# Reordering the tasks, the first transfers and the weight loads of an attention kernel with a woven MLP

## The chip, the cores and the metric

One core of a Trainium2 chip runs the whole program. The metric is the device time of one execution in microseconds (us). The kernel before took 422.31 us, the median of three runs (421.84 to 426.07); the run that was profiled took 421.53.

The engines: TensorE (PE in the profile; PEld is its weight load), VectorE (DVE), ScalarE (ACT), GpSimd (POOL) and SyncE (SP), which here only issues transfers. A suffix q (ACTq, SPq, POOLq) means that engine's sequencer.

## The reference

```python
def _attn_ref(q, k, v, s):            # 8 batches x 8 heads, sequence 576, head size 64
    scores = scale * q @ k^T
    cum = cumsum(max(s, 0))
    scores += minimum(-(cum_i - cum_j), 0), causal
    attn = softmax(scores)
    return attn @ v
def _moe_ref(x, w_in, w_out):         # 4608 tokens, 512 -> 2048 -> 512
    h = x @ w_in
    return (h * clip(h + 3, 0, 6) / 6) @ w_out
```

The output of the attention, all heads of a token side by side, is the input x of the MLP.

## The kernel before

Two heads of one batch form a pair; there are 32. For each pair q and k are loaded in f32, cast to f16 on GpSimd (`cast_qk`), transposed in two groups on TensorE, and copied out of PSUM by VectorE. The scores of a head come in four PSUM banks. ScalarE takes the exponential of each and GpSimd zeroes the upper triangle (`mask`). `attend` multiplies by v, and `x_transpose` writes the normalised result into the MLP's input.

```python
S = psum.tile([128, 512], F32, tag="S", bufs=3)   # score banks, transposes and x transposes share it

def att_tasks(p):
    tasks = []
    def pre():
        if p + 2 < NP: load_aug(p + 2)            # decay rows, read back from DRAM
        if p + 3 < NP: load_pair(p + 3)           # q, k, v
        if p + 1 < NP:
            cast_qk(p + 1)
            cast_v(p + 1)
        for load, c in weights[2 * p:2 * p + 2]:  # eight chunks, pairs 0 to 3, issued by GpSimd
            load(c)
    tasks.append((pre, 0))
    if p + 1 < NP: tasks.append((lambda: transpose_group(p + 1, 0), 640))
    # ... four scores_bank of head 2p, attend(2p - 1)
    # ... transpose_group(p + 1, 1), four scores_bank of head 2p + 1
    # ... x_transpose(p - 1), attend(2p)
```

In the traces here each engine's instructions come in the order in which the program writes them. The attention of pairs 0 to 4 runs alone at the head. Then a weaver mixes attention tasks with MLP tasks by the costs given with the tasks: `m1` is four matmuls into ph, a ReLU on ScalarE (trl) and a product on VectorE; `m2` is four matmuls into po. When attention ends, the MLP runs alone.

The softmax here doesn't subtract the row's maximum and nothing guards it: scores larger than these inputs give would overflow.

## Time and profile before

| Stage | From | To | What runs |
|---|---|---|---|
| head | 0 | 58.0 | loads, attention of pairs 0 to 4; first exponential at 19.8 |
| first weave | 58.0 | 95.0 | pairs 5 to 8 with the first block of m1 |
| rest | 95.0 | 419.6 | attention woven with m1 and m2, then the MLP alone |

The times are where the first ph and the first po start in TensorE's timeline. TensorE is busy for 366.7 of 419.6 us. Nearly all its room is in the first two stages; the lines are in the prediction.

### The profile page before, as it was taken

To read this page: it belongs to the slowest core of one execution; us is meant where nothing else is said; L and a number is where in the kernel's file an instruction comes from. 1 tells how busy PE (TensorE), PEld (TensorE's weight loads), DVE (VectorE), ACT (ScalarE), POOL (GpSimd) and SP (SyncE) were. 2 spreads that over 40 slices of the span, in tenths; PEclk is the share of its full clock that TensorE was granted. 3 is DMA by queue.
4 is the path that set the end of the run, shared out by engine and by line. 5 is a ranking of instruction groups with operands and counts; after the bars stand their busy time and mean duration, and the time that the engine had idled before them with its cause. 6 is when DMAs were issued, how large, how long until landed. Compare 5 with 4: busy or idle time off the path is not lost.

```text
span 419.6 us, 8151 instructions
## 1 busy us (share of the span) xinstructions
PE 366.7 (87%) x3008; PEld 210.0 (50%) x3008; DVE 226.1 (54%) x412; ACT 213.2 (51%) x407; POOL 142.7 (34%) x336
## 2 busy tenths in 40 slices
PE   1274677879999999999999999999999999999985
PEld 0153445545555555555555555555555554444432
DVE  4233346666666666666666666666656644454521
ACT  6153347675555555555555555555555644444400
POOL 3284644444343444444444444444434210000000
PEclk9988589999999999999999999999999999999999
DMA  6999999645554554555555455455501000101011
GB/s 131 166 207 199 200 192 187 124 85 108 111 110 110 111 109 111 111 111 108 111 111 109 111 111 109 112 114 112 110 27 51 26 27 25 52 25 51 25 75 51
DMA packets 123511, 43.38 MB, mean 103 GB/s; under 512 B 114192, under 2 KB 118672, under 8 KB 123472
## 3 DMA queue, kind: packets, MB, share of 16 engines
q1 hardware_dynamic: 119248, 38.68, 42.1%
q0 software_dynamic: 4224, 4.19, 6.3%
q8 instruction: 23, 0.38, 0.4%
q14 instruction: 16, 0.13, 0.1%
HBM read 37.32 MB, written 9.73 MB: 112 GB/s over the span
## 4 chain that ended last, share of the span: by engine, by line
PE 68%; DVE 10%; DMA 6%; ACT 5%; issue 4%; POOL 3%; SPq 3%; POOLq 0%; ACTq 0%
PE po L327 26%; PE ph L309 25%; PE S L203 8%; PE O L252 6%; DVE osb L336 4%; ACT trl L317 3%; DMA t<-in_k_dram 3%; PE pT L163 3%; DVE kT L174 2%; ACT Pm L211 2%; PE pX L277 2%; POOL t L150 2%; DVE qT L173 2%; DMA v_f<-in_v_dram 1%; SPq L132 1%
## 5 line engine op out<-in xcount | busy, mean ns | idle before, releaser
L317 ACT ACTIVATE trl<-ph,bias 128x512 f32<-128x512 f32 x144 | 99.1, 688 | 139.0 <-PE ph L309 138.4
L318 DVE SCALAR_TENSOR_TENSOR gT<-trl,ph 128x512 f16<-128x512 f32 x144 | 99.1, 688 | 99.8 <-ACT trl L317 98.3
L327 PE MATMUL po<-w_out_sb,gT 128*128 128x512 f16 x576 | 144.5, 379 | 2.3 <-DVE osb L336 2.3
L309 PE MATMUL ph<-xT,w_in_sb 128*128 128x512 f16 x576 | 146.3, 379 | 0.0
L216 POOL TENSOR_SCALAR_AFFINE_SELECT Pm<-Pm 128x128 f16<-128x128 f16 (+2 forms) x256 | 78.1, 310 | 168.0 <-ACT Pm L211 156.5
L211 ACT ACTIVATE Pm<-S 128x384 f16<-128x384 f32 (+2 forms) x256 | 112.6, 507 | 44.0 <-PE S L203 43.7
L203 PE MATMUL S<-qT,kT 128*128 128x320 f16 (+4 forms) x448 | 74.2, 273 | 15.6 <-DVE kT L174 9.8
L327 PEld LDWEIGHTS <-gT 128*128 128x128 f16 x576 | 52.2, 98 | 54.7 <-issue 3.2
L309 PEld LDWEIGHTS <-w_in_sb 128*128 128x128 f16 x576 | 51.6, 97 | 52.5 <-issue 9.2
L203 PEld LDWEIGHTS <-kT 128*128 128x128 f16 x448 | 40.4, 102 | 28.7 <-issue 5.5
L173 DVE COPY qT<-pT 64x640 f16<-64x640 f16 x64 | 28.5, 445 | 47.5 <-PE pT L163 47.5
L163 PE MATMUL pT<-ident,t 128*128 128x128 f16 x288 | 28.8, 233 | 26.6 <-POOL t L150 26.6
L252 PEld LDWEIGHTS <-Pm 128*128 128x128 f16 x960 | 40.4, 100 | 17.8 <-POOL Pm L216 4.1
L252 PE MATMUL O<-v_h,Pm 128*128 128x65 f16 x960 | 42.7, 197 | 3.5 <-POOL Pm L216 3.4
L150 POOL CAST t<-t 128x1152 f16<-128x1152 f32 x32 | 37.0, 1158 | 14.9 <-DMA t<-in_k_dram 14.7
L163 PEld LDWEIGHTS <-t 128*128 128x128 f16 x288 | 21.9, 104 | 39.3 <-POOL t L150 27.9
L336 DVE TENSOR_SCALAR osb<-po 128x512 f32<-128x512 f32 x36 | 24.7, 685 | 13.2 <-PE po L327 13.2
L174 DVE COPY kT<-pT 64x640 f16<-64x640 f16 x64 | 29.4, 459 | 0.9
L155 POOL CAST v_h<-v_f 128x640 f16<-128x640 f32 x32 | 23.1, 722 | 12.4 <-DMA v_f<-in_v_dram 11.2
L264 DVE TENSOR_TENSOR xs<-O,r 128x640 f16<-128x640 f32 x32 | 26.4, 824 | 1.1
L262 DVE RECIPROCAL r<-O 128x10 f32<-128x10 f32 x32 | 7.1, 220 | 19.8 <-PE O L252 19.8
L277 PEld LDWEIGHTS <-xs 128*128 128x128 f16 x160 | 11.7, 98 | 11.8 <-issue 5.7
(23 smaller groups left out, 49.1 us busy)
## 6 DMA issues: line engine op xcount, KB each, us to landing
t<-in_q_dram SPq DMA_DIRECT2D x32, 288.0 KB
t<-in_k_dram SPq DMA_DIRECT2D x32, 288.0 KB
out_dram<-osb SPq DMA_DIRECT2D x36, 256.0 KB
v_f<-in_v_dram SPq DMA_DIRECT2D x64, 128.0 KB
w_in_sb<-in_moe_w_in_dram POOLq DMA_DIRECT2D x4, 512.0 KB, 8.7
w_out_sb<-in_moe_w_out_dram POOLq DMA_DIRECT2D x4, 512.0 KB, 8.7
v_f<-in_v_dram SPq DMA_DIRECT2D x32, 32.0 KB
kT<-kaug_scratch SPq DMA_DIRECT2D x32, 6.8 KB
```

The costliest lines, as they stand in the source:

```text
L150: nc.gpsimd.tensor_copy(out=t, in_=qk_f.pop(p))
L163: nc.tensor.matmul(out=pT[:, (t - t0) * 128:(t - t0 + 1) * 128], lhsT=src[:, t, :, :], rhs=ident, is_transpose=True, start=(t == t0), stop ...
L174: nc.vector.tensor_copy(out=kT[0:64, sl, c0:c0 + n], in_=pT[64:128, 0:n])
L203: nc.tensor.matmul(out=S[:, c:c + hi - lo], lhsT=kT[:, sl, off + 128 * kt:off + 128 * (kt + 1)], rhs=qT[:, sl, off + lo:off + hi], start=( ...
L211: nc.scalar.activation(out=P[:, p0:p0 + n], in_=S[:, 0:n], func=AF.Exp, scale=0.125, bias=0.0)
L216: nc.gpsimd.affine_select(out=view, in_=view, pattern=pattern, compare_op=ALU.is_ge, fill=0.0, base=0, channel_multiplier=-1,)
L252: nc.tensor.matmul(out=O[:, hh, qt * VW:qt * VW + D + 1], lhsT=P[:, c:c + 128], rhs=v_h[:, sl, hh, kt, 0:D + 1], start=(qt == 0), stop=(qt ...
L309: nc.tensor.matmul(out=ph, lhsT=w_in_sb[:, kc, f * 128:(f + 1) * 128], rhs=xT[:, kc, n * 512:(n + 1) * 512], start=(kc == 0), stop=(kc == ...
L317: nc.scalar.activation(out=trl, in_=ph, func=AF.Relu, bias=bias3[:, 0:1], scale=1.0)
L318: nc.vector.scalar_tensor_tensor(out=gT[n][:, f, :], in0=trl, scalar=6.0, in1=ph, op0=ALU.min, op1=ALU.mult)
L327: nc.tensor.matmul(out=po, lhsT=gT[n][:, f, t4 * 128:(t4 + 1) * 128], rhs=w_out_sb[:, f, :], start=(f == 0), stop=(f == NF - 1),)
L336: nc.vector.tensor_scalar_mul(out=osb, in0=po, scalar1=1.0 / 6.0)
```

## The change

The diff below is shortened: lines in brackets and `...` stand for what is left out. Its intent is a shorter head and fewer stalls of TensorE before transposes: pair p's scores go ahead of pair p+1's transposes, the cast of q and k goes between the masks, the loads of pairs 1 and 2 are issued before the round trip of the decay rows, part of the first transfers goes to ScalarE's queue, weights load later, and ten zero matmuls are to keep TensorE's clock up. The last line moves the point where the weave begins, so that it still follows `x_transpose`.

```diff
-    nc.sync.dma_start(out=amask[64:128], ...)
-    nc.sync.dma_start(out=ident, in_=ident_dram.ap())
+    nc.scalar.dma_start(out=amask[64:128], ...)
+    nc.scalar.dma_start(out=ident, in_=ident_dram.ap())
 ...
-    load_pair(0)
-    (kaug, qaug written to DRAM by nc.sync)
-    load_aug(0); load_aug(1)
-    load_pair(1); load_pair(2)
+    load_qk(0, nc.sync)
+    load_v(0, nc.scalar)
+    load_qk(1, nc.sync); load_v(1, nc.sync)
+    load_qk(2, nc.sync); load_v(2, nc.sync)
+    mask_rows(0)
+    (kaug, qaug written to DRAM by nc.scalar)
+    mask_rows(1)
+    load_aug(0, nc.scalar); load_aug(1, nc.scalar)
+    mask_rows(2)
 ...
+    for i in range(10):
+        nc.tensor.matmul(out=pw, lhsT=warm[:, 0:128], rhs=warm, ...)
-    weights = [w_in 0..3, w_out 0..3]            # two a pair from pair 0
+    weights = {1: [w_in 0], 2: [w_in 1, w_in 2], 3: [w_in 3],
+               4: [w_out 0, w_out 1], 5: [w_out 2, w_out 3]}
 ...                                              # tasks of pair p, in their new order
+        tasks = [(loads, 0)]
+        for bi in range(4):
+            tasks.append((lambda bi=bi: scores_bank(2 * p, bi), 400))
+            if bi == 1 and more:
+                tasks.append((lambda: cast_qk(p + 1), 0))
+        # attend(2p - 1) at 1200 in place of 1600, then transpose_group(p + 1, 0),
+        # four scores_bank(2p + 1), cast_v(p + 1), x_transpose(p - 1),
+        # transpose_group(p + 1, 1) at 640 in place of 512, attend(2p)
 ...
-                cut.append(len(att_all) - 1)
+                cut.append(len(att_all) - 2)
```

More of the change, by code (lines that the diff above doesn't have):

```diff
@@ L80 @@
     nc.sync.dma_start(out=s_sb, in_=s.rearrange("b h t -> (b h) t"))
-    nc.sync.dma_start(out=amask[64:128], in_=amask_dram.ap().rearrange("i p t -> p i t"))
-    nc.sync.dma_start(out=ident, in_=ident_dram.ap())
+    nc.scalar.dma_start(out=amask[64:128], in_=amask_dram.ap().rearrange("i p t -> p i t"))
+    nc.scalar.dma_start(out=ident, in_=ident_dram.ap())
     s8 = work.tile([NH, SEQ], F32, tag="s1", bufs=1)
@@ L106, with mask_rows @@
     nc.gpsimd.memset(Pm[:, :, 1600:PW], 1.0)
-    for i, dst in enumerate((kT, qT)):
-        for sl in range(NS):
+    def mask_rows(sl):
+        for i, dst in enumerate((kT, qT)):
             nc.scalar.activation(
@@ L118, with load_qk @@
     qk_h = {}
-    def load_pair(p):
+    def load_qk(p, eng):
         b, h0 = (2 * p) // H, (2 * p) % H
-        t = work.tile([128, NTR, 2, D], F32, tag="qkf", bufs=3)
+        t = work.tile([128, NTR, 2, D], F32, tag="qkf", bufs=3, name=f"qkf{p}")
         for i, src in enumerate((q, k)):
-            nc.sync.dma_start(
+            eng.dma_start(
                 out=t[:, :, i, :],
@@ L129, in load_pair, with load_v @@
             )
+        qk_f[p] = t
+    def load_v(p, eng):
+        b, h0 = (2 * p) // H, (2 * p) % H
         sl = p % NS
         for hh in range(2):
-            nc.sync.dma_start(
+            eng.dma_start(
                 out=v_f[:, sl, hh, 0:4, :],
@@ L135, in load_pair @@
             )
-        nc.sync.dma_start(
+        eng.dma_start(
             out=v_f[0:64, sl, :, 4, :],
@@ L139, in load_pair, with load_aug @@
         )
-        qk_f[p] = t
-    def load_aug(p):
+    def load_aug(p, eng):
         sl = p % NS
         c0 = p * W2
-        nc.sync.dma_start(out=kT[64:67, sl, 0:W2], in_=kaug_dram[:, c0:c0 + W2])
-        nc.sync.dma_start(out=qT[67:68, sl, 0:W2], in_=qaug_dram[:, c0:c0 + W2])
+        eng.dma_start(out=kT[64:67, sl, 0:W2], in_=kaug_dram[:, c0:c0 + W2])
+        eng.dma_start(out=qT[67:68, sl, 0:W2], in_=qaug_dram[:, c0:c0 + W2])
     def cast_qk(p):
@@ L341 @@
     nc.vector.memset(bias3, 3.0)
-    load_pair(0)
-    nc.sync.dma_start(
+    warm = cpool.tile([128, 512], F16, tag="c_warm")
+    nc.vector.memset(warm, 0.0)
+    load_qk(0, nc.sync)
+    load_v(0, nc.scalar)
+    load_qk(1, nc.sync)
+    load_v(1, nc.sync)
+    load_qk(2, nc.sync)
+    load_v(2, nc.sync)
+    mask_rows(0)
+    nc.scalar.dma_start(
         out=kaug_dram.rearrange("r (h t) -> h r t", h=NH), in_=kaug
     )
-    nc.sync.dma_start(out=qaug_dram.rearrange("r (h t) -> h (r t)", h=NH), in_=qaug)
@@ L349 @@
-    load_aug(0)
-    load_aug(1)
-    load_pair(1)
-    load_pair(2)
+    nc.scalar.dma_start(out=qaug_dram.rearrange("r (h t) -> h (r t)", h=NH), in_=qaug)
+    mask_rows(1)
+    load_aug(0, nc.scalar)
+    load_aug(1, nc.scalar)
+    mask_rows(2)
     cast_qk(0)
     cast_v(0)
-    weights = [(load_w_in, c) for c in range(4)] + [(load_w_out, c) for c in range(4)]
+    pw = psum.tile([128, 512], F32, tag="M", bufs=2, name="pw")
+    for i in range(10):
+        nc.tensor.matmul(
+            out=pw, lhsT=warm[:, 0:128], rhs=warm, start=(i == 0), stop=(i == 9)
+        )
@@ L358, in att_tasks, with loads @@
+    weights = {
+        1: [(load_w_in, 0)],
+        2: [(load_w_in, 1), (load_w_in, 2)],
+        3: [(load_w_in, 3)],
+        4: [(load_w_out, 0), (load_w_out, 1)],
+        5: [(load_w_out, 2), (load_w_out, 3)],
+    }
     def att_tasks(p):
-        tasks = []
-        def pre():
+        def loads():
             if p + 2 < NP:
-                load_aug(p + 2)
+                load_aug(p + 2, nc.sync)
             if p + 3 < NP:
-                load_pair(p + 3)
-            if p + 1 < NP:
-                cast_qk(p + 1)
-                cast_v(p + 1)
-            for load, c in weights[2 * p:2 * p + 2]:
-                load(c)
@@ L373, in att_tasks @@
-        tasks.append((pre, 0))
-        if p + 1 < NP:
+                load_qk(p + 3, nc.sync)
+                load_v(p + 3, nc.sync)
+            for load, c in weights.get(p, []):
+                load(c)
+        more = p + 1 < NP
+        tasks = [(loads, 0)]
[3 more added lines that the diff above has]
+                tasks.append((lambda: cast_qk(p + 1), 0))
+        if p > 0:
+            tasks.append((lambda: attend(2 * p - 1), 1200))
@@ L375, in att_tasks @@
+        if more:
             tasks.append((lambda: transpose_group(p + 1, 0), 640))
         for bi in range(4):
-            tasks.append((lambda bi=bi: scores_bank(2 * p, bi), 400))
-        if p > 0:
-            tasks.append((lambda: attend(2 * p - 1), 1600))
-        if p + 1 < NP:
-            tasks.append((lambda: transpose_group(p + 1, 1), 512))
-        for bi in range(4):
             tasks.append((lambda bi=bi: scores_bank(2 * p + 1, bi), 400))
+        if more:
+            tasks.append((lambda: cast_v(p + 1), 0))
@@ L384, in att_tasks @@
         if p > 0:
             tasks.append((lambda: x_transpose(p - 1), 640))
-        tasks.append((lambda: attend(2 * p), 1600))
+        if more:
+            tasks.append((lambda: transpose_group(p + 1, 1), 640))
+        tasks.append((lambda: attend(2 * p), 1200))
         return tasks
@@ L423 @@
             if p % 4 == 0:
-                cut.append(len(att_all) - 1)
-    att_all += [(lambda: attend(NH - 1), 1600), (lambda: x_transpose(NP - 1), 640)]
+                cut.append(len(att_all) - 2)
+    att_all += [(lambda: attend(NH - 1), 1200), (lambda: x_transpose(NP - 1), 640)]
     cut.append(len(att_all))
```

## The prediction

> **What bounds the kernel now.** I read the page first. Its slices show one thing at once: TensorE is at 90% or more from the tenth slice on, and only the first nine (10.5 us each) have room.
>
> ```profile
> PE   1274677879999999999999999999999999999985
> PEclk9988589999999999999999999999999999999999
> GB/s 131 166 207 199 200 192 187 124 85 108 111 110 110 111 109 111 111 111 108 111 111 109 111 111 109 112 114 112 110 27 51 26 27 25 52 25 51 25 75 51
> ```
>
> The timeline of TensorE gives the stages: the first scores at 19.3 us, the first hidden-layer matmuls (ph) at 58.0, the first output matmuls (po) at 95.0. Up to 58 attention of pairs 0 to 4 runs alone; 58 to 95 weaves pairs 5 to 8 with the first MLP block; from 95 attention and two MLP blocks are woven. The table by stretch, for these stages:
>
> ```profile
> core 0: us, PE busy (x) PEld busy (x) DVE busy (x) ACT busy (x) POOL busy (x), PEclk, DMA share, GB/s
> 16.00:58.00 42.00, 25.81 (x255) 18.98 (x256) 14.27 (x31) 18.30 (x40) 24.15 (x50) 0.76 1.22 206
> 58.00:95.00 37.00, 28.93 (x301) 18.14 (x299) 23.57 (x44) 23.38 (x49) 18.78 (x47) 1.00 0.69 133
> 95.00:340.00 245.00, 237.72 (x2100) 139.08 (x2098) 148.39 (x275) 139.78 (x279) 96.29 (x231) 1.00 0.45 99
> 340.00:419.60 79.60, 73.09 (x353) 32.93 (x350) 33.50 (x51) 24.07 (x35) 0.00 (x0) 0.99 0.12 43
> ```
>
> So 16 to 58 is a transfer stage (206 GB/s, DMA share above 1, no compute engine above 62%), at a granted clock of 0.76. 58 to 95 is bound by no engine's busy time: it must be a chain. Then TensorE is the bound, with 7.3 us of it spare at most. The waits of the first 92 us name the chains:
>
> ```profile
> PE pT L163 <- POOL t L150: 26.6, 10, 9.4
> POOL t L150 <- DMA t<-in_k_dram: 14.7, 4, 7.5
> POOL v_h L155 <- DMA v_f<-in_v_dram: 11.2, 3, 5.4
> ```
>
> TensorE stands before each pair's transposes for GpSimd's cast of q and k; in pairs 3 to 6 that cast, or v's, waits for a transfer. In 58 to 95 the transfer has landed and the cast is only late in GpSimd's queue: it stands behind all eight masks of the pair before, as the chain that ended last shows:
>
> ```profile
> 76.48 0.98 ACT Pm L211 x2
> ...
> 77.51 0.24 POOL Pm L216
> ...
> 78.09 1.15 POOL t L150
> 79.24 0.05 issue
> 79.29 0.45 PE pT L163 x5
> ```
>
> The same five steps come every 8.8 us (70.5, 79.3, 88.1). Past 95 the waits view has one TensorE wait of note:
>
> ```profile
> PE S L203 <- DVE kT L174: 7.9, 21, 0.6
> ```
>
> **What the Trainium skill says.** "DMA: Bandwidth & Descriptors", section "Issuing engines are not separate DMA queues", says that transfers from ScalarE, SyncE and GpSimd run on the same 16 engines and interleave, so another issuer saves only issue time. I therefore give no bandwidth to ScalarE's queue; the trace before shows the sharing only between SyncE and GpSimd (206 GB/s together). The same page, section "SWDGE vs HWDGE vs iDMA", has GpSimd building its own descriptors: here each weight issue holds GpSimd 0.76 to 0.79 us. "TensorE: Matmul & The Clock Gate", Part 1, gives half clock after an idle window and full clock after about 3.4 us of activity. The trace agrees: the clock is 0.50 in 40 to 50 us, after idle gaps of 3.2 and 1.4 us, and five transposes take 0.71 us there against 0.45 warm.
>
> **The change part by part.**
>
> Weights. By bytes a pair of q, k, v is 0.885 MB (3 x 288 KB), 4.3 us at 206 GB/s; a weight chunk is 0.52 MB as counted, 2.6 us. Before, all eight chunks (20.5 us) fall in 20 to 47 us, beside pairs 3 to 5. After, four input chunks come in pairs 1 to 3, the output chunks in pairs 4 and 5. They still cost GpSimd 0.8 us apiece.
>
> Start. The first scores waited for pair 1's transposes (k of pair 1 issued only at 13.2, behind the cumulative rows' round trip, landed 17.5, cast to 18.7). After, pairs 0 to 2 are issued before that trip and pair 0's scores come first. What remains: rows ready on VectorE at 8.4; written through DRAM in 2.9 us (3.5 to 5 estimated beside the loads), read back in about 2.5; ScalarE, which now issues and waits, then does its last two mask copies (2.2 us) before the first exponential. That gives first scores at 16 to 18, I take 16.7, against 19.3. The ten zero matmuls sit at about 9 to 13 us, where TensorE is idle; they cost nothing and may keep the clock up.
>
> Pairs alone. With transfers out of the way I follow one pair, T = first scores, with these durations: four score banks 0.70 us, attend 0.47, five transposes 0.28, four 0.23, x transposes 0.28; exponentials 0.45 to 0.6; masks 0.41, 0.29, 0.24, 0.29; cast 1.15. Exponential 1 starts at T+0.42, 2 ends at T+1.46; its mask ends at T+1.82; the cast, now second after two masks, ends at T+2.95; transposes to T+3.28; the other head's four exponentials run T+3.7 to T+5.65; x transposes wait for a bank (the second exponential, T+4.8) and, with group two and attend, end at T+5.9. So 5.9 us a pair, more where weight issues hold the masks back: +0.45 for one, +1.25 for two. From 16.7: pairs 0 to 4 take 5.9, 6.35, 7.15, 6.35 and 6.3 (to its x transposes), to 48.7; half a us for copies and some cold clock make the first ph 49.5 against 58.0. Transfers keep ahead of this: k of pair 5 should land at about 36 and is wanted at 45.
>
> Pairs 5 to 8 with block 0. Now a ph (0.86 us) stands between bank 0 and bank 1, and ScalarE must do its ReLU (0.69) before exponential 2: that ends at T+2.41, mask at 2.77, cast at 3.90, transposes from 3.94. TensorE would be there at 2.89, so it waits 1.05. Later the x transposes wait some 0.9 us for a PSUM bank, which the second head's exponential 2 frees late, again behind a ReLU. TensorE's work is 6.5 us (four ph 3.45, scores 1.4, attend 0.94, transposes 0.8); with 1.95 of waits the period is 8.45 against 8.8. Four pairs: 34 us. First po at 83.5 to 84, against 95.0: 11 us gained. The earlier cast is worth little here, because ScalarE still serves in order.
>
> Steady part. TensorE gets at the transposes at T+3.75 (a po more stands before them), the cast is through at 3.94: 0.2 us of wait in place of the 0.36 for kT, whose evictions now have a po behind them. In a pair of 10.53 us (the same m1 pieces recur at 163.68, 174.21, 184.73) that is 0.17, by 23 pairs 4 us. The tail from 340 is untouched.
>
> Sum: 11 + 4 = 15, less a little for what I can't follow; 422.3 - 15 = 407, and since several unknowns (clock, weave) lean to the better side, I say 406.
>
> **Rivals.**
> (a) *The head shrinks to its transfers.* If chains overlap better than I draw them, only bytes limit: to the first po some 13.9 MB at 206 GB/s, 70 us with 2 us of start. That would gain 25 and give about 395. For it: the transfer stage is saturated now. Against: in 58 to 95 the DMA share is 0.69 and pairs still take 8.8.
> (b) *The wait moves.* The cast after two masks is late for TensorE also in the steady part: if exponential 2 slips 0.3 us (a ReLU more ahead), each pair waits 0.5 in place of 0.36, 23 x 0.15 = 3.5 us lost, and only 8 are gained: 414.
> (c) *The start gets worse.* ScalarE now issues eleven transfers (0.2 to 0.9 us each on SyncE) ahead of its exponentials, and waits for the DRAM round trip while pairs 1 and 2 load. If both queues' issues share one generator, first scores come at 19 and the gain is 2.5 us less: 409.
> (d) *Nothing.* If the head's gain were given back at 95 to 340, the time would stay. TensorE is 97% busy there and not fed by what the head leaves behind, so I see no way for that.
>
> **Range and chances.** Middle 406. The upper end is (b) and (c) together, 414; the lower is nine tenths of the way to (a), 396. Faster by over 2% needs less than 413.9: nearly the whole range, 0.92. Within 2%: 0.07. Slower: 0.01.
>
> **What would show it right or wrong.** The first exponential at about 17 (19.8 before); the first ph near 49.5; the first po near 84; a period of about 8.4 us between; DMA share below 1 past 40 us; in the waits of the head the transposes still behind GpSimd's cast but with hardly any wait of the cast for k; the granted clock of 20 to 50 us near 1; past the first po, TensorE's wait for kT gone and one for the cast of about 0.2 us a pair in its place; pair period 10.3 to 10.4. A first po at 75 or less makes the chain model wrong and (a) right; a pair period of 10.6 or more makes (b) right.

## The result

| | Before | After |
|---|---|---|
| time, median of four runs | 423.99 us | 403.25 us (403.11 to 403.31) |
| profiled span | 419.6 us | 401.6 us |
| first exponential | 19.8 | 16.8 |
| first ph | 58.0 | 48.4 |
| first po | 95.0 | 83.1 |
| from first po to the end | 324.6 | 318.5 |

The ratio is 0.951 (95% interval 0.945 to 0.957). A ratio here is taken over the fast runs of the same rounds, so it is not quite the ratio of the medians quoted. Executions over 1.5% slower than the fastest of the same kernel are left out of the means. The profiled spans differ by 18.0 us: 11.9 before the first po and 6.1 after it.

From the page of the changed kernel, the slices (10.0 us each) that answer to those of before:

```profile
PE   1576788899999999999999999999999999999985
PEclk9779899999999999999999999999999999999999
DMA  9999998955555545555555555554300001010111
GB/s 176 211 165 197 205 218 179 194 104 115 117 117 117 116 118 115 118 116 115 114 114 114 115 111 113 116 113 105 67 26 29 28 26 54 26 52 28 40 65 53
```

TensorE reaches 90% in the ninth slice instead of the tenth. The transfers are dense up to 80 us: the bytes have not become fewer, but they hardly stop anybody any more. The clock is still down in the second and third slices. The table by stretch, cut at the same events (first ph, first po):

```profile
core 0: us, PE busy (x) PEld busy (x) DVE busy (x) ACT busy (x) POOL busy (x), PEclk, DMA share, GB/s
16.00:48.40 32.40, 21.65 (x251) 15.97 (x252) 13.70 (x29) 17.46 (x41) 23.60 (x53) 0.82 1.06 187
48.40:83.10 34.70, 29.42 (x299) 17.99 (x297) 23.20 (x44) 24.39 (x50) 17.87 (x42) 0.98 0.97 183
83.10:322.00 238.90, 238.71 (x2101) 137.59 (x2099) 149.15 (x276) 139.37 (x280) 94.52 (x232) 1.00 0.46 102
322.00:401.60 79.60, 73.14 (x361) 33.20 (x357) 33.56 (x51) 23.88 (x35) 0.00 (x0) 1.00 0.12 43
```

The head's stretch falls from 42.0 to 32.4 us, the first weave only from 37.0 to 34.7. The waits of the first 90 us show what is left (engine, line, releaser: us in total, times, longest):

```profile
PE pT L166 <- POOL t L153: 10.7, 9, 2.1
...
POOL t L153 <- DMA qkf<-in_k_dram: 6.2, 1, 6.2
```

GpSimd waits for k once only, for pair 0's at the very start: its waits for k and v come to 6.2 us in place of 25.9 (14.7 and 11.2, of which 13.4 are for k of pairs 0 and 1). TensorE's wait for the cast before the transposes is 10.7 us in place of 26.6, but it did not become shorter pair by pair. Two of the ten waits of before are the start itself:

```profile
9.44 1.14 PE L163 MATMUL pT<-ident,t 128*128 128x128 f16 x9 [9.44 <-POOL t L150]
18.75 0.71 PE L163 MATMUL pT<-ident,t 128*128 128x128 f16 x5 [8.17 <-POOL t L150]
```

Without these, TensorE waited 9.0 us in eight waits before and 10.7 in nine after, where the start is listed under the zero matmuls (8.9 us) and the first scores (2.9). The head gained by its earlier start and by transfers that come in time, not by a shorter wait for the cast. The chain in the first weave now reads like this (start, us, what):

```profile
59.65 0.50 ACT Pm L214
...
60.21 0.41 POOL Pm L219
60.62 1.05 issue
...
61.70 0.29 POOL Pm L219
61.99 1.11 POOL t L153
...
63.14 0.45 PE pT L166 x5
```

The cast stands behind two masks in place of eight. The 1.05 us between the masks are not GpSimd's: ScalarE's ReLU of the woven m1 (trl) runs ahead of the second exponential, as its own timeline shows:

```profile
59.65 0.49 ACT L214 ACTIVATE Pm<-S 128x384 f16<-128x384 f32 x1 [0.23 <-PE S L206]
60.45 0.69 ACT L320 ACTIVATE trl<-ph,bias 128x512 f32<-128x512 f32 x1 [0.31 <-PE ph L312]
61.04 1.29 ACT L214 ACTIVATE Pm<-S 128x512 f16<-128x512 f32 x3
```

The next transposes come at 71.64: 8.5 us a pair, 8.8 before. Here too TensorE's gain is not at the transposes (idle of 0.40 us shown a pair before, 0.56 after); it is at a score bank that waits for kT, 0.63 before and 0.16 after.

In the steady part the wait of 20 score banks for kT, the first fence (kernel before, from 95 us), is gone. In the changed kernel only the weight loads ahead of the transposes wait, the second fence:

```profile
PE S L203 <- DVE kT L174: 7.3, 20, 0.4
```

```profile
PEld L166 <- POOL t L153: 10.0, 20, 0.5
```

Neither number is the time lost, and it is worth seeing why. Here is TensorE's timeline of before around one such wait (start, busy, what; idle before it):

```profile
145.43 0.55 PE L203 MATMUL S<-qT,kT 128*128 128x192 f16 x4
146.34 0.30 PE L203 MATMUL S<-qT,kT 128*128 128x320 f16 x1 [0.36 <-DVE kT L174]
```

and of after at the transposes:

```profile
108.88 1.02 PE L312 MATMUL ph<-xT,w_in_sb 128*128 128x512 f16 x4
109.92 0.45 PE L166 MATMUL pT<-ident,t 128*128 128x128 f16 x5
```

The four score matmuls of before have 896 columns, which take about 0.40 us where nothing stops them (the six before another bank have 1280 and take 0.56 from start to start). The next bank starts 0.91 us after them, so 0.51 is lost, although 0.36 is shown as idle. The busy times listed overlap what follows: four ph are listed with 1.02 to 1.03 us, yet where nothing waits the next instruction starts 0.86 us after their start. After, four ph take 0.86 from start to start when nothing waits; here it is 1.04, so 0.18 is lost, though no idle time of TensorE is shown at all and 0.5 is shown for the weight load. All 20 pairs are alike: 0.91 in each before, 1.03 to 1.04 in each after. From 0.51 to 0.18 is 0.33 us a pair, by 20 pairs 6.6, against the 6.1 measured after the first po. "Perfetto Trace Analysis", section "Tensor Engine Instruction (MATMUL, LD_WEIGHTS)", says that the profiler estimates the end of such instructions rather than observing it, and this trace agrees: starts are what to subtract.

### The profile page after: what moved, and what is told of

It is laid out like the page before. It is cut to its first block, busy times and chain, and to the rows that moved or that the text cites. A ratio compares the mean times of both kernels' runs of the same rounds, so it can differ in the third digit from the quotient of the medians.

```text
span 401.6 us, 8143 instructions
## 1 busy us (share of the span) xinstructions
PE 367.5 (91%) x3018; PEld 206.7 (51%) x3018; DVE 226.3 (56%) x413; ACT 212.8 (53%) x407; POOL 139.3 (35%) x336
## 4 chain that ended last, share of the span: by engine, by line
PE 83%; POOL 6%; ACT 3%; DMA 2%; issue 2%; DVE 2%; ACTq 0%; SPq 0%; POOLq 0%
PE po L330 31%; PE ph L312 29%; PE S L206 9%; PE O L255 6%; PE pT L166 5%; PE pX L280 2%; POOL t L153 2%; POOL Pm L219 2%; ACT Pm L214 2%; DMA qaug_scratch<-qaug 1%; DMA s_sb<-in_s_dram 1%; DMA v_f<-in_v_dram 1%; DVE osb L339 1%; POOL v_h L158 1%; POOL w_in_sb L292 1%
## 5 line engine op out<-in xcount | busy, mean ns | idle before, releaser
L214 ACT ACTIVATE Pm<-S 128x384 f16<-128x384 f32 (+2 forms) x256 | 114.0, 504 | 77.1 <-PE S L206 76.3
L219 POOL TENSOR_SCALAR_AFFINE_SELECT Pm<-Pm 128x128 f16<-128x128 f16 (+2 forms) x256 | 77.0, 307 | 175.1 <-ACT Pm L214 155.0
L206 PE MATMUL S<-qT,kT 128*128 128x320 f16 (+4 forms) x448 | 72.6, 268 | 5.4 <-ACT qT L110 2.9
L206 PEld LDWEIGHTS <-kT 128*128 128x128 f16 x448 | 42.2, 100 | 37.5 <-ACT qT L110 3.0
L255 PEld LDWEIGHTS <-Pm 128*128 128x128 f16 x960 | 37.9, 98 | 6.7 <-issue 1.2
L255 PE MATMUL O<-v_h,Pm 128*128 128x65 f16 x960 | 40.9, 194 | 0.0
L153 POOL CAST t<-qkf 128x1152 f16<-128x1152 f32 x32 | 36.8, 1150 | 6.2 <-DMA qkf<-in_k_dram 6.2
L166 PE MATMUL pT<-ident,t 128*128 128x128 f16 x288 | 27.6, 225 | 11.0 <-POOL t L153 10.7
L166 PEld LDWEIGHTS <-t 128*128 128x128 f16 x288 | 19.7, 100 | 31.3 <-POOL t L153 23.5
L339 DVE TENSOR_SCALAR osb<-po 128x512 f32<-128x512 f32 x36 | 24.8, 689 | 13.8 <-PE po L330 13.2
L288 DVE COPY xT<-pX 128x576 f16<-128x576 f16 x32 | 14.5, 452 | 5.1 <-PE pX L280 5.0
```

The lines of the kernel that those rows point to most:

```text
L153: nc.gpsimd.tensor_copy(out=t, in_=qk_f.pop(p))
L166: nc.tensor.matmul(out=pT[:, (t - t0) * 128:(t - t0 + 1) * 128], lhsT=src[:, t, :, :], rhs=ident, is_transpose=True, start=(t == t0), stop ...
L206: nc.tensor.matmul(out=S[:, c:c + hi - lo], lhsT=kT[:, sl, off + 128 * kt:off + 128 * (kt + 1)], rhs=qT[:, sl, off + lo:off + hi], start=( ...
L214: nc.scalar.activation(out=P[:, p0:p0 + n], in_=S[:, 0:n], func=AF.Exp, scale=0.125, bias=0.0)
L219: nc.gpsimd.affine_select(out=view, in_=view, pattern=pattern, compare_op=ALU.is_ge, fill=0.0, base=0, channel_multiplier=-1,)
L255: nc.tensor.matmul(out=O[:, hh, qt * VW:qt * VW + D + 1], lhsT=P[:, c:c + 128], rhs=v_h[:, sl, hh, kt, 0:D + 1], start=(qt == 0), stop=(qt ...
```

## The experiments

Eleven runs were made, two of them of the changed kernel itself as controls. All gave correct results. In each group the kernel before ran in the same rounds; its median was 425.6 to 426.0 us there. The stage times are from one profile each.

| Run | Median us | Ratio to before | First exp. | First ph | First po | First po to end |
|---|---|---|---|---|---|---|
| before (the profiled run) | 421.53 | 1 | 19.8 | 58.0 | 95.0 | 324.6 |
| after_again | 404.16 | 0.951 | 17.0 | 48.8 | 84.0 | 318.6 |
| no_zero | 403.74 | 0.950 | 17.2 | 48.7 | 83.7 | 318.4 |
| one_queue | 406.64 | 0.957 | 20.0 | 51.7 | 86.6 | 318.5 |
| weights_early | 411.05 | 0.966 | 18.1 | 56.7 | 90.8 | 318.5 |
| b_weights | 414.36 | 0.976 | 19.7 | 51.1 | 88.4 | 324.6 |
| b_order | 413.62 | 0.973 | 16.8 | 62.1 | 96.2 | 318.6 |
| b_start | 420.69 | 0.990 | 17.3 | 53.7 | 93.8 | 324.6 |
| cast_first | 397.23 | 0.935 | 16.7 | 44.8 | 79.2 | 314.8 |
| after_third | 403.88 | 0.950 | 16.8 | 48.5 | 83.6 | 318.6 |
| spread | 401.49 | 0.945 | 17.3 | 46.8 | 80.9 | 318.5 |
| spread_cast_first | 391.12 | 0.920 | 16.8 | 41.5 | 75.9 | 314.9 |

The last column depends on the order of tasks alone: 324.6 with the old one, 318.5 with the new, 314.8 with the cast first. Everything else acts before the first po.

**after_again and after_third: the controls.** No edit.

> Control: the changed kernel again, to have its time in the same rounds as the next two. Every theory: 403.3 us, within 0.3%.

> Control for the next two: the changed kernel once more, 403 to 404.5 us.

404.16 and 403.88 us, as expected. With the first 403.25, three medians of one kernel differ by up to 0.9 us, so smaller differences between runs are not read here.

**no_zero: without the ten zero matmuls.**

```diff
-    warm = cpool.tile([128, 512], F16, tag="c_warm")
-    nc.vector.memset(warm, 0.0)
-    for i in range(10):
-        nc.tensor.matmul(out=pw, lhsT=warm[:, 0:128], rhs=warm, ...)
```

> The changed kernel without the ten zero matmuls and their memset. Theory: they end at 12.9 us, TensorE then idles 2.9 us before the first scores, and the profile of the changed kernel shows cold transposes again at 19.3 us (0.71 us for five), so they buy nothing: within 0.5 us of the control. Rival: they keep part of the first 20 us warm, and without them the cold stretch ends later than 28 us: 1 to 3 us slower.

403.74 us against 404.16: they buy nothing. TensorE's timeline without them:

```profile
9.54 1.14 PE L166 MATMUL pT<-ident,t 128*128 128x128 f16 x9 [9.54 <-POOL t L153]
16.65 1.49 PE L206 MATMUL S<-qT,kT 128*128 128x256 f16 x7 [5.97 <-DMA qT<-qaug_scratch]
19.70 0.71 PE L166 MATMUL pT<-ident,t 128*128 128x128 f16 x5 [1.56 <-POOL t L153]
```

and in the changed kernel, which has them:

```profile
12.76 0.67 PE L166 MATMUL pT<-ident,t 128*128 128x128 f16 x9
...
19.34 0.71 PE L166 MATMUL pT<-ident,t 128*128 128x128 f16 x5 [1.56 <-POOL t L153]
```

Nine transposes right after the zero matmuls take 0.67 us in place of 1.14, so TensorE is warm then. Five take 0.45 warm; at 19.34 they take 0.71, as without the zero matmuls at 19.70. The granted clock of the changed kernel is 1.00 from 14 to 15 us, 0.90 from 15 to 16 and 0.50 from 16 to 18: the warmth bought is gone when the scores start at 16.3. "TensorE: Matmul & The Clock Gate", Part 4, says that transposes do not count as busy in the same way; between the last zero matmul at 12.9 and the first scores at 16.3 only transposes ran, which fits, though no run here separates that from plain idling. (The transposes at 25.95 in this profile are slow, with 0.67 us, but in both controls they take 0.45 at that place, as in no_zero, so that is no effect of the zero matmuls.)

One warning about the clock in these profiles. In no_zero it reads 1.00 from 15 to 40 us, although the transposes at 19.70 were slow. A 1.00 in the first tens of us is thus no proof of a warm TensorE; the durations of its own instructions decide.

**one_queue: all first transfers on SyncE.**

```diff
-    nc.scalar.dma_start(...)      # mask tables, identity, v of pair 0, rows out and back
+    nc.sync.dma_start(...)        # same program order
```

> The changed kernel with the seven kinds of ScalarE issue (mask tables, identity, v of pair 0, the rows' round trip) put on SyncE's queue, in the same program order. Theory: what the second queue gives is place in line, not bandwidth: the rows' write would be issued behind all loads of pairs 0 to 2, at about 18 us in place of 8.6, the first exponential comes at 24 to 26 in place of 16.8, and the time is 409 to 412. Rival: all queues share the same engines, so the bytes land at the same times: 403 to 404.

406.64 us, 2.5 more than the control: between both. The rows' write is issued here, in the timeline of SyncE:

```profile
14.31 0.61 SPq L356 DMA_DIRECT2D kaug_scratch<-kaug  x1
```

and in the changed kernel here:

```profile
8.57 0.63 ACTq L356 DMA_DIRECT2D kaug_scratch<-kaug  x1
```

It is 5.7 us later, not the 9.4 that I had expected: SyncE was through with the loads of three pairs sooner than I had reckoned, at 14.2. The first exponential is 3.0 us later, and the time follows. What the second queue gives is a place in the order of issue: here the write stood behind the issuing of ten loads, which kept SyncE busy from 6.27 to 14.19 us.

**weights_early: the old weight schedule in the changed kernel.**

```diff
-    weights = {1: [w_in 0], 2: [w_in 1, w_in 2], 3: [w_in 3], 4: [w_out 0, w_out 1], 5: [w_out 2, w_out 3]}
+    weights = {0: [w_in 0, w_in 1], 1: [w_in 2, w_in 3], 2: [w_out 0, w_out 1], 3: [w_out 2, w_out 3]}
```

> The changed kernel with the weights back where they were: two chunks a pair in pairs 0 to 3. Theory: bytes bound the head again. From about 17 us, pairs 3 to 5 (13 us) and eight chunks (20.5 us) must land before k of pair 5 is cast: first ph at 52 to 54 in place of 48.6, first po at 87 to 88, the cast of q and k waiting for k by several us again, time 407 to 409. Rival: with the new order the chain of exponentials and casts binds alone and the place of the weights is worth nothing: 403 to 404.5.

411.05 us, some 7 more than the changed kernel, so the loss is larger than I had expected, and the rival falls. The first ph comes at 56.7 in place of 48.4 to 48.8. TensorE's timeline shows the transposes of pair 5, which stand in pair 4's tasks, behind a late k:

```profile
53.92 0.71 PE L166 MATMUL pT<-ident,t 128*128 128x128 f16 x5 [6.78 <-POOL t L153]
```

and GpSimd's cast before it waited 5.41 us for k of pair 5. The 0.71 us tell that TensorE had gone cold as well. A chunk may also cost more than the 2.6 us that its counted bytes gave: on the page of the kernel before, the transfers of GpSimd's queue take 6.3% of the 16 DMA engines' span for eight chunks, which makes 3.3 us a chunk. That is an estimate; no run isolates it.

**b_weights: only the weights, in the kernel before.**

```diff
-    weights = [w_in 0..3, w_out 0..3]    # two a pair, pairs 0 to 3
+    weights = {1: ..., 5: ...}           # as in the changed kernel
```

> The kernel before with the weights in the later pairs, nothing else. Theory: the transfer stage goes, the chain behind all eight masks stays: first exponential 19.8 as before, pairs at 6.4 to 7.4 us (the first two pairs of before), first ph at 51 to 53, weave still 8.8 a pair, first po at 87 to 89, steady pairs 10.5: 6 to 8 us gained, 415 to 418. Rival: the weights were hidden and the pairs are chain-bound anyway: under 2 us gained.

414.36 us. The profile does what was expected: first ph at 51.1, first po at 88.4, the rest unchanged. The span is 6.6 us shorter than that of the profiled run before, while the ratio of 0.976 to the runs of the same rounds means some 10 us. The difference is in the kernel before: its profiled run was one of its faster ones. GpSimd's waits for k and v between 19 and 60 us fall from 12.4 to 0.4 us, so the gain is that of the transfers and not of the later issuing alone. The granted clock of the stretch from its first scores to its first ph reads 1.00, but the transposes in it were slow for longer than in the kernel before, until after 32.76:

```profile
17.00:51.10 34.10, 25.09 (x256) 18.31 (x257) 14.27 (x31) 18.45 (x40) 25.14 (x55) 1.00 1.12 197
```

```profile
32.76 0.71 PE L163 MATMUL pT<-ident,t 128*128 128x128 f16 x5 [0.36 <-POOL t L150]
...
40.38 0.45 PE L163 MATMUL pT<-ident,t 128*128 128x128 f16 x5 [0.96 <-POOL t L150]
```

The kernel before was warm at 32.55 already but cold again at 43.32 and 52.16, after attend had waited 3.22 us. That such falls make the scatter of the kernel before is not shown.

**b_order: the new order alone.** The changed kernel with the start and the weights of before and without zero matmuls.

> The changed kernel's order of tasks (scores ahead, casts between masks, casts of v late) with the start and the weights of before and no zero matmuls. Theory: steady pairs at 10.2 (7 us gained), weave at 8.5 (1 us), the head bound by bytes as before, but started 3 us earlier since pair 0's scores no longer wait for pair 1's k: first exponential at 15 to 17, first ph at 54 to 56: 409 to 413 in all. Rival: the head's order frees its DMA slots later and eats it: 415 or more.

413.62 us, a hair above the range. The steady part and the weave came as expected (318.6 from the first po; 34.1 us of weave), the head did not: the first ph came at 62.1 (in a run 2.9 us slower than the median), in place of 54 to 56. GpSimd's timeline shows both ends of it:

```profile
9.88 1.63 POOL L293 DMA_DIRECT2D w_in_sb<-in_moe_w_in_dram  x2
...
51.74 1.14 POOL L154 CAST t<-qkf 128x1152 f16<-128x1152 f32 x1 [9.81 <-DMA qkf<-in_k_dram]
```

In the kernel before, the first weights stood in GpSimd's queue behind pair 1's cast:

```profile
19.84 1.63 POOL L289 DMA_DIRECT2D w_in_sb<-in_moe_w_in_dram  x2
```

The new order takes that cast out of their way. They are issued at 9.9 us, before the k of pair 1 at 13.2, and the last of the eight by 41.3 in place of 46.8; the cast that waits 9.81 us is pair 4's, which before was done by 43.3. That the early chunks starve the pairs is argued from these times. Its gain is shown in the weave and the rest. Between the two profiles the head loses 4.1 us; but this run was 2.3 us above the mean of its kernel and the profiled run of before 3.7 below its own, so that the head loses anything on average is not shown.

**b_start: the new start alone.** The changed start with the order and weights of before and no zero matmuls.

> The start of the changed kernel (pairs 1 and 2 issued ahead, rows on ScalarE's queue) with the order and the weights of before and no zero matmuls. Theory: the queues are no longer idle from 9 to 13 us, so the bytes of the head land 3 to 4 us sooner and nothing else moves: first ph at 54 to 55, steady pairs 10.5: 419 to 421 if before is 424. Rival: pair 0's scores still stand behind pair 1's transposes and the head is bound by its weights: no gain, 423 to 425.

420.69 us, as expected; ratio 0.990. In its profile the first ph came at 53.7, 4.3 us earlier, but only 1.2 of it reached the first po: the weave took 40.1 us, with v of one pair 7.84 us late for its cast. In this profile the early weights take back in the weave most of what the start gives in the head.

**cast_first: the cast ahead of all masks of the pair.**

```diff
         tasks = [(loads, 0)]
+        if more:
+            tasks.append((lambda: cast_qk(p + 1), 0))
         for bi in range(4):
             tasks.append((lambda bi=bi: scores_bank(2 * p, bi), 400))
-            if bi == 1 and more:
-                tasks.append((lambda: cast_qk(p + 1), 0))
```

> The changed kernel with the cast of q and k moved from after bank 1 to the very front of the pair, ahead of all its masks. Theory (TensorE waits at the transposes for a cast that stands behind exponential 2 and its mask): the wait of about 1.6 us a pair in the head and 0.56 in the weave goes, pairs alone take about 5 us in place of 6 to 6.8, first po near 77, time 396 (394 to 399). Rival 1: the masks come 1.15 us later and attend waits for them instead: 402 to 405. Rival 2: transfers become the bound of the head: DMA share stays above 1 to 60 us, gain under 3 us.

397.23 us, 6.9 less than the control: 4.8 before the first po and 3.8 after it in the profiles, whose run was 1.5 us faster than the median. Attend never waits for the masks. The steady gain is the 0.18 us a pair that the changed kernel loses at the transposes: by 20 pairs 3.6. In the weave the pairs that wait for no transfer now take 7.77 us in place of 8.5. In the head and the weave a part of rival 2 came true. The longest wait is now this:

```profile
60.68 0.45 PE L166 MATMUL pT<-ident,t 128*128 128x128 f16 x5 [2.90 <-POOL t L153]
```

There GpSimd's cast waits 5.20 us for k, which was loaded beside the four output chunks (issued at 39.3 and 46.1). The zero matmuls are still in this kernel, and here its first five transposes, at 17.76, take 0.44 us: scores and transposes that start early enough do find TensorE warm. What that is worth was not run.

**spread: thinner and later weights in the changed kernel.**

```diff
-    weights = {1: [w_in 0], 2: [w_in 1, w_in 2], 3: [w_in 3], 4: [w_out 0, w_out 1], 5: [w_out 2, w_out 3]}
+    weights = {1: [w_in 0], 3: [w_in 1], 4: [w_in 2], 5: [w_in 3], 6: [w_out 0, w_out 1], 7: [w_out 2, w_out 3]}
```

> The changed kernel with the weights later still and thinner: one input chunk in pairs 1, 3, 4 and 5, two output chunks in pairs 6 and 7. Theory: bytes no longer bind the head of the changed kernel, so only GpSimd's own time for issuing (two chunks less in pair 2, one less in pair 4, 0.75 us each, of which some 0.4 to 0.7 are on the chain) comes back: first ph 1.2 to 2.2 us earlier, time 1.2 to 2.2 us under the control. Rival: bytes still bind the head: 4 us or more under it. Other rival: the output chunks land too late for the first po (wanted at about 82 us): slower than the control.

401.49 us, 2.4 under the control, just above the range; the first ph came 1.7 us earlier. Three issues less ahead of it give 0.6 us each, which GpSimd's own time (0.75 us an issue) can give. The size speaks against bytes as the bound of the changed kernel's head, and so does its profile, where no cast waits for k after pair 0.

**spread_cast_first: both together, without the zero matmuls.**

> The cast ahead of the masks, the thinner weights and no zero matmuls together. Theory: in the run with the cast first alone TensorE waited 1.7 and 2.9 us for casts that waited for k, behind two and three chunks of weights; with these spread both waits go, first ph at 42 to 43, first po at 73.5 to 76, time 5 to 7 us under the 397.2 of the cast alone: 390 to 392. Rival: the transfers, 13.9 MB to the first po, are the floor already at about 70 us plus what they start late: first po at 78 or more, 396 to 397.

391.12 us, ratio 0.920 (interval 0.915 to 0.924), the best and 3% under the changed kernel. The parts help each other: 6.1 us under cast_first, while thinner weights gave 2.4 to the changed kernel. First ph at 41.5 and first po at 75.9, both close to the expectation. But the waits for k did not go: two casts in the weave wait 2.2 and 3.9 us, at a DMA share of 1.09, so the rival, transfers as the next floor, came true in part. The six runs fall into two groups, 388.7 to 390.0 and 392.3 to 392.8, and the profiled one is of the slower; why is open.

## Why the prediction was right

The predicted time was 406 with a range of 396 to 414; 403.25 was measured. Step by step:

*What bounds the kernel.* Right. The head of before was bound by bytes: b_weights moves only the weights, gains 6.9 us of head and all but ends the waits for k and v after 19 us, and weights_early loses about 8 by putting them back. The weave was bound by a chain: in weights_early, where the bytes are through by then (DMA share 0.71 in that stretch), it takes 34.1 us, hardly less than the 34.7 of the changed kernel with a share of 0.97.

*Start.* First scores at 16.7 were predicted and came at 16.3. The rows' write took 3.9 us beside the loads (8.57 to 12.44), in the estimated 3.5 to 5. The zero matmuls cost nothing, as said. "May keep the clock up" was wrong: the warmth ended at about 16 us. The sign of a clock near 1 from 20 us on failed too (0.82 from 16 to 48.4), and it was a poor sign, since no_zero reads 1.00 with slow transposes. Also read too kindly was "the trace agrees": in the kernel before the clock fell at 39.0 us, inside the gap of 3.2 us and before that of 1.4, and stayed at 0.50 until 56, although TensorE was busy for 10.4 of the 15 us from 40 to 55.

*Pairs alone.* Predicted 5.9, 6.35, 7.15, 6.35 and 6.3, in all 32.05; measured from the starts of the first score bank 6.4, 7.0, 6.5, 6.0 and 5.7, in all 31.6. That the sum is so close is in part luck: single pairs are off by 0.3 to 0.7 us both ways. The first two ran cold, for which the sum had only half a us at its end, and the later ones cost less than drawn. How the time falls on the pairs also varies: in after_again it is 6.4, 6.1, 7.5 and 6.0 for the first four. First ph 49.5 predicted, 48.4 measured.

*Pairs 5 to 8.* The period of 8.45 was measured as 8.5, and the weave as 34.7 in place of 34. That the earlier cast is worth little here because ScalarE serves in order shows in the chain: the second exponential behind the ReLU is the 1.05 us gap. By starts TensorE loses about 0.7 us before the transposes (1.05 predicted), 0.9 before the x transposes (0.9 predicted) and 0.3 at kT (none predicted), so the sum of 1.95 is right and one of its terms is not. The work terms add up to 6.59 and not to 6.5. First po predicted at 83.5 to 84, measured at 83.1.

*Steady part.* The direction was right, the term too small: 0.17 us a pair by 23 pairs, 4 us, against 6.1. The wait for the cast was 0.18, as predicted (0.2). The mis-sized term is the old wait for kT: I took the 0.36 us that the profile shows as idle before the bank. By starts it lost 0.51. The pair fell from 10.53 to 10.22 (x transposes at 93.09 and 103.31).

*A sign that failed.* "DMA share below 1 past 40 us" did not come: it was 1.22 from 40 to 50 and 1.23 from 50 to 60, and only then below 1. It was the wrong sign to choose. The same bytes in a shorter time must keep the engines fuller; what told the truth was that after pair 0 no cast waited for k.

*Rivals.* (a), a head that shrinks to its transfers, did not come here. With the cast first it begins to: in spread_cast_first the waits of casts for k come to 14.1 us, 6.7 of them for pair 0, and its first po at 75.9 is not far from the 70 drawn for (a). (b) did not: the wait cost 0.18 us and the pair fell to 10.22, where (b) asked for 10.6. (The range was mis-added: (b) alone gives 414, with (c) it would be 416; and 25 us off 422.3 give 397 for (a), not 395.) (c) did not: the first exponential came at 16.8. (d) fell.

What stays open: why the kernel before scatters by 1.5% while the changed one does not (its runs have mean granted clocks of 0.96 to 0.98, but spread_cast_first scatters by 1.05% at 0.997 to 1.000, so the clock alone does not explain it); and what each part is worth in every combination, for they are not additive. From the ratios and a mean of before near 425 us, weights, order and start alone give about 10, 11 and 4.5 us, together 26, and the whole change 21.

## What to carry to other kernels

When an engine stands before a product of another engine's queue, look at what that queue executes first, and write the product as far ahead of its consumer as its input allows: one line moved further (the cast before the masks) gave another 6.9 us. Spread large loads that are needed late so thinly that the loads needed soon keep their lead; a transfer engine that is full is no bound while nobody waits for it. Measure a matmul wait from start to start, not by the idle time shown, and take a clock that reads 1.00 early in a profile for warm only if the instructions are fast.

## What the Trainium skill lacked or had wrong

- "DMA: Bandwidth & Descriptors", section "Issuing engines are not separate DMA queues", says that a second issuer only saves issue time, usually small. The kind is right; here it was not small. With one issuer the rows' write was issued at 14.3 in place of 8.6 us, and the kernel took 2.5 us more.
- On the same page I found no figure for two queues issuing at once. Beside ScalarE's issues SyncE issued its last load of pair 2 at 14.50 us; alone, with more to issue ahead of it, at 13.59. The cause is not isolated.
- "TensorE: Matmul & The Clock Gate", Part 1, has nothing on how the start of a clock record reads: in no_zero the granted clock is 1.00 from 15 to 40 us, while five transposes at 19.70 take 0.71 us; in b_weights it is 1.00 from 17.0 to 51.1, with 0.71 at 32.76.
- "Perfetto Trace Analysis" says that ends of matmuls are estimated, but not what this does to idle times: 0.36 us shown as idle was 0.51 lost, and 0.18 lost showed as none.
